# Two state-space convolutions with a gate: units of 64 channels, an inverse turned through DRAM, and a first stage in array quarters

## The chip, the cores and the metric

The kernel runs on one core of a Trainium2 chip. The metric is device time in microseconds of one execution; the median of three runs of the kernel before is 520.16 us (519.94 to 523.69). Profiles are of one execution, recorded by the hardware profiler. Engines are named as in the profile: PE (TensorE), DVE (VectorE), ACT (ScalarE), POOL (GpSimd), and SP, whose queue issues all DMA transfers here.

## What is computed

The input `x` has 2048 time steps and 512 channels, all in fp32. Two diagonal state-space systems, A and B, each with 128 complex states per channel, give a convolution kernel each, and the outputs are mixed by a gate that depends on the time step alone:

```python
P = exp(logdA[:, :, None] * l)             # 512 channels x 128 states x 2048 steps
K = einsum("dn,dnl,dn->dl", Cc, P, dB).real  # system A; system B has 2 * (C dt . P).real
y = irfft(rfft(u, 2L) * rfft(K, 2L))[:L] + u * Dskip
g = sigmoid((x * gate_w).sum(-1))           # one number per time step
out = g * a + (1 - g) * b
```

No library transform exists on the chip, so both kernels `K` are summed up by matmuls over the states, and the convolution is done by a discrete transform in two stages, also of matmuls, with an inverse in two stages.

## The kernel before, in words

The 512 channels are cut into four quarters `q` of 128. A **unit** is one quarter of one system (`k` = 0 for A, 1 for B), so there are eight units. A unit goes through these steps:

- `params_t`, `params_c` (once per quarter): small operations of 128 states x 256 that turn the raw parameters into phases (integers, so that they wrap), decay exponents and a complex factor. Most of it is on DVE, some on ACT and POOL.
- `anchors`, `weights`: ACT fills a table `AB` of exponentials; POOL multiplies part of it by the factor.
- `chunk`, eight times per unit, 16 channels each. POOL makes two phase products in a tile `x` (L562 and L553) and two products of exponentials in a tile `E` (L573, L581). ACT takes four sines and cosines of 128x512 into PSUM banks (L591, L592, L595, L599), with one Abs of 128x1024 between (L593). DVE multiplies them with `E` into `Qt`, `Pt`, `Ct` and `Dt` (L603, L606, L616, L621, L612); for 31 of the 64 chunks `Dt` is made on POOL instead, from a sine in SBUF (`scs`). PE sums over the states (`products`, L638: four column strips of 32), adds the skip tap (L647), and ACT copies the result to `K`.
- stage one (`stage1`, `put`, L681): matmuls of `K` with a small cosine table into `F`, 256 columns at a time in two column halves; a copy by DVE or ACT (L692, L694).
- `stage2`: forward matmuls with `Gw` (L703), a product with the transformed input read back from DRAM as `U` (L764, L767 on DVE), inverse matmuls with `Tw` (L775, L776), and a copy back into `F` by ACT (L781).
- `final`: DVE transposes `F` in place in 32x32 blocks (L797), PE does the last inverse stage (L803), and the result is multiplied by the gate on its way out of PSUM: system A's by ACT or DVE (L817, L819), stored to DRAM as `w0`, and loaded again for system B, where DVE multiplies and adds (L880).

The input itself goes through stage one and the forward matmuls once per quarter (`stage1_u`, `stage2_u`), and its transform is written to DRAM (`ud`). `gate` sums `x * gate_w` by matmuls (L902) and takes the sigmoid.

What sets the order: every operation is recorded with an engine, a cost, a due time and the buffers that it reads and writes. `Plan.run` plays a clock over these costs; whenever an engine is free, the ready operation with the earliest due time goes next. The outcome is a fixed order of instructions per engine, in which they are then written. The numbers at the top of the file (`LAG`, `FSP`, `TO` and so on) shift the due times; `SLOTS` and `CAPS` say how many tiles of each kind there are. Each engine runs its instructions in that order, waiting on semaphores. PSUM has eight banks of 128x512; before, all eight are one pool `ps`, of which the sines may hold four.

## Time and profile before

| | |
|---|---|
| median of three runs | 520.16 us |
| profiled execution, span from first to last instruction | 519.0 us |
| PE busy | 453.8 us, 7732 matmul records |
| DVE busy | 444.5 us, 740 instructions |
| ACT busy | 418.1 us, 786 instructions |
| POOL busy | 423.1 us, 368 instructions |
| moved by DMA | 74.71 MB, 35747 packets |

Every fp32 matmul of the program appears as two records, each with its weight load (PEld). Busy times of the four engines overlap; none says by itself what the span would be without it. A line of the table of groups gives the source line, the engine, the operation, the tiles written and read, the shape and the count, then the busy time and the mean of one, then the idle time of the engine right before these instructions and what ended it.

### The profile page before, as it was taken

What the parts mean: (1) busy time and instruction counts of PE and PEld (TensorE: products, weight loads), DVE (VectorE), ACT (ScalarE), POOL (GpSimd) and SP (SyncE); (2) the same over time, 40 slices, a digit from 0 to 9 for tenths busy, and PEclk for the clock granted to TensorE, in tenths of its full rate; (3) what the DMA queues carried; (4) which work ended last, traced back from release to release, by engine and by line L of the source; (5) the groups of instructions that cost most, each with busy time, mean ns of one, the idle gap of its engine ahead of it and who ended that gap; (6) DMA issues with size and microseconds to landing.
All of it is one profiled execution on the core that took longest, in us unless ns stands there. A gap on an engine that the chain in (4) does not pass through costs nothing.

```text
span 519.0 us, 18350 instructions
## 1 busy us (share of the span) xinstructions
PE 453.8 (87%) x7732; PEld 393.0 (76%) x7732; DVE 444.5 (86%) x740; ACT 418.1 (81%) x786; POOL 423.1 (82%) x368
## 2 busy tenths in 40 slices
PE   2788999879879868979999999996889799999993
PEld 1687989778768646769877898995769679987971
DVE  6658898887959879999999999999998978999854
ACT  4778797797999769989999968876999998675233
POOL 4376999987999998986998999997799989994003
PEclk9879999889969999988999999997899989999999
DMA  8728438624205454435235664440255063433632
GB/s 296 316 74 263 124 105 246 190 88 157 83 3 164 162 180 136 153 103 164 83 124 163 194 221 147 153 124 12 75 158 179 13 215 103 135 123 133 201 116 81
DMA packets 35747, 74.71 MB, mean 144 GB/s; under 512 B 3792, under 2 KB 4176, under 8 KB 35408
## 3 DMA queue, kind: packets, MB, share of 16 engines
q1 hardware_dynamic: 35664, 73.54, 43.7%
q8 instruction: 60, 0.98, 0.8%
q14 instruction: 23, 0.19, 0.1%
HBM read 53.60 MB, written 19.92 MB: 142 GB/s over the span
## 4 chain that ended last, share of the span: by engine, by line
PE 40%; DVE 21%; ACT 20%; issue 6%; DMA 5%; POOL 5%; SPq 0%; POOLq 0%; DVEq 0%; ACTq 0%
PE ps L681 9%; PE ps L703 8%; PE ps L775 7%; PE ps L776 6%; PE ps L638 6%; PE ps L803 3%; ACT AB L496 2%; DMA AB<-in_prm 2%; ACT ps L591 2%; ACT x L593 2%; DVE F L797 2%; DVE Ct L621 2%; DVE Pt L616 2%; DVE z L767 2%; DVE F L692 2%
## 5 line engine op out<-in xcount | busy, mean ns | idle before, releaser
L581 POOL TENSOR_TENSOR E<-AB 128x1024 f32<-128x1024 f32 x64 | 125.2, 1958 | 0.1
L703 PE MATMUL ps<-F,c_g 128*128 128x128 f32 x768 | 105.6, 286 | 15.9 <-DVE fi L453 9.0
L703 PEld LDWEIGHTS ps<-F,c_g 128*128 128x128 f32 x768 | 94.8, 195 | 24.4 <-DVE fi L453 9.5
L775 PE MATMUL ps<-z,c_t 128*128 128x128 f32 x512 | 105.5, 289 | 5.7 <-DVE Pt L616 2.6
L776 PE MATMUL ps<-z,c_t 128*128 128x128 f32 x512 | 101.6, 281 | 0.1
L775 PEld LDWEIGHTS ps<-z,c_t 128*128 128x128 f32 x512 | 79.9, 197 | 13.8 <-DVE z L767 3.4
L562 POOL TENSOR_TENSOR x<-pi,c_tm 128x512 int32<-128x512 int32 x64 | 67.8, 1060 | 20.8 <-ACT ps L595 18.7
L616 DVE TENSOR_TENSOR Pt<-ps,E 128x1024 f32<-128x1024 f32 x64 | 77.8, 1216 | 4.8 <-PE ps L638 2.9
L776 PEld LDWEIGHTS ps<-z,c_t 128*128 128x128 f32 x512 | 79.8, 197 | 0.8 <-DVE z L767 0.7
L681 PE MATMUL ps<-w,K 128*64 128x128 f32 x1024 | 68.9, 284 | 10.2 <-ACT K L657 6.3
L681 PEld LDWEIGHTS ps<-w,K 128*64 128x64 f32 x1024 | 57.6, 141 | 19.5 <-ACT K L657 8.2
L573 POOL TENSOR_TENSOR E<-AB 128x512 f32<-128x512 f32 x64 | 68.4, 1070 | 4.2 <-ACT AB L496 2.4
L638 PE MATMUL ps<-Pt,Ct 128*32 128x64 f32 x2048 | 66.1, 227 | 5.5 <-DVE Ct L621 3.4
L553 POOL TENSOR_TENSOR x<-gh 128x512 int32<-128x512 int32 x64 | 68.3, 1068 | 1.9 <-ACT ps L599 1.8
L593 ACT ACTIVATE x<-x 128x1024 f32<-128x1024 int32 x64 | 67.9, 1061 | 1.7
L638 PE MATMUL ps<-Qt,Dt 128*32 128x64 f32 x2048 | 64.4, 224 | 0.0
L781 ACT COPY F<-ps 128x512 f32<-128x512 f32 x64 | 37.2, 586 | 33.8 <-PE ps L776 28.5
L638 PEld LDWEIGHTS ps<-Pt,Ct 128*32 128x32 f32 x2048 | 47.3, 113 | 18.9 <-DVE Ct L621 5.4
L764 DVE TENSOR_TENSOR z<-ps,U 128x512 f32<-128x512 f32 x64 | 43.5, 680 | 20.1 <-DMA U<-ud 14.0
L496 ACT ACTIVATE AB<-al 128x128 f32<-128x128 f32 (+1 forms) x160 | 55.1, 528 | 1.4 <-DVE ps L452 1.1
L638 PEld LDWEIGHTS ps<-Qt,Dt 128*32 128x32 f32 x2048 | 49.2, 114 | 0.0
L603 DVE TENSOR_TENSOR Qt<-ps,E 128x512 f32<-128x512 f32 x64 | 43.4, 679 | 5.3 <-POOL E L581 3.8
(114 smaller groups left out, 869.5 us busy)
## 6 DMA issues: line engine op xcount, KB each, us to landing
U<-ud SPq DMA_DIRECT2D x64, 512.0 KB, 3.9
ud<-z SPq DMA_DIRECT2D x32, 256.0 KB, 3.5
U<-in_u SPq DMA_DIRECT2D x16, 256.0 KB, 4.0
ud<-z SPq DMA_DIRECT2D x32, 128.0 KB, 3.4
U<-in_uT SPq DMA_DIRECT2D x8, 512.0 KB, 4.1
c_t<-in_c_t SPq DMA_DIRECT2D x1, 3072.0 KB, 14.9
w<-st SPq DMA_DIRECT2D x12, 256.0 KB, 2.6
st<-w SPq DMA_DIRECT2D x12, 256.0 KB, 3.0
```

Source lines behind the costliest of these rows:

```text
L496: A.activation(dst()[..., i], src(), AF.Exp, scale=sg * float(t0 + dt * i))
L553: G.tensor_tensor(xi()[:, :, 1, :].rearrange("n c (a b) -> n c a b", a=4), t[:, :, 0:4].unsqueeze(3).to_broadcast([P, NCK, 4, 8]), t[:, :, ...
L562: lambda: G.tensor_tensor(xi()[:, :, 0, :], d["piv"]()[:, k, ch, 0].unsqueeze(2).to_broadcast([P, NCK, NJ]), tm[:, 0:NJ].unsqueeze(1).to_b ...
L573: G.tensor_tensor(Ev()[:, :, 0, :].rearrange("n c (a b) -> n c a b", a=4), A1()[:, ch, ::-1].unsqueeze(3).to_broadcast([P, NCK, 4, 8]), BB ...
L581: G.tensor_tensor(Ev()[:, :, 1:3, :].rearrange("n c w t -> n c (w t)"), AA()[:, ch].rearrange("n c w a -> n (c w) a").unsqueeze(3).to_broa ...
L593: op("A", 1.02, e, lambda: A.activation(x.t, x.v(dt=I32), AF.Abs), w=[x])
L616: lambda: V.tensor_tensor(qv(Pt), tv(cf).unsqueeze(2).to_broadcast([P, NCK, 2, NJ]), Ev()[:, :, 0:2, :], ALU.mult),
L638: T.matmul(K4[32 * b : 32 * b + 32, g, :], tv(lw)[:, 4 * g + b, :], qv(rw)[:, 4 * g + b].rearrange("n h t -> n (h t)"), start=(lw is Ct an ...
L681: T.matmul(b.t[64 * d : 64 * d + 64, 128 * g : 128 * g + 128], Kv[:, g, :], w1[:, d, :], start=True, stop=True,)
L703: T.matmul(pairs(b.t[:, NCH * mm : NCH * mm + NCH]), Gw[:, 4 * mg + mm, :], Fv(F)[:, :, 4 * mg + mm, :], start=True, stop=True,)
L775: T.matmul(hb.t[:, cs], Tw[:, m, 0:128], Z1.t[:, cs], start=True, stop=False)
L776: T.matmul(hb.t[:, cs], Tw[:, m, 64:192], Z2.t[:, cs], start=False, stop=True)
```

## The change

The planner (`Plan`) stays. What it is given changes throughout:

- **Units.** A unit is now 64 channels of both systems, still 128 columns and still eight units. `U` is loaded for 64 channels and used for both systems: 36 loads of 512 KB where there were 64.
- **Gate.** Since `g*a + (1-g)*b = b + g*(a-b)`, PE subtracts B's kernel from A's while it is still in PSUM (`neg`, L669), and the second half of a unit's columns holds `a-b`. The last inverse stage multiplies B's columns by `w1i` and the others by `wg`, which is `w1i` times the gate for each time step (POOL, L898), and adds both in PSUM. The products with the gate on the way out, and `w0`, are gone; a plain copy goes to the output (L855, L857).
- **Turn.** The result of stage two is copied to `st` and written to DRAM (`wt`, 64 writes), and read back with rows in the order that the last stage needs (L827). The transposes on DVE are gone.
- **Sines.** Each chunk takes one sine and one cosine of 128x1024 over two banks (L606, L608) into two tiles `sd` of two banks each; four banks are left as `ps`. `Dt` is always on DVE, as one product with half of `Qt` (L614); the cosine products are written in place into `E` (L624, L629), which has three tiles where there were two.
- **First stage.** 512 columns of `K` at a time are multiplied in quarters of the array: 32 matmuls of 64 rows and 64 columns into two banks (L692).
- **Last unit.** It is transformed in two halves of 64 columns (`SPLIT`), so that its matmuls of stage two move 64 columns each, and written and read in pieces of 64 elements.
- The parameter steps are shorter by five DVE operations per quarter, with two sign operations on POOL instead; `F` has two tiles and a separate tile `X` in place of three; all of `u` is transformed early, and the gate too; the costs given to the planner are other numbers.

The core of the diff:

```diff
-    "F": (4096, 3), "AB": (28 * NCH, 2), "x": (1024, 2), "E": (1536, 2), "Qt": (1024, 2), "Dt": (512, 2),
...
-    "st": (512, 3), "p": (256, 5), "dtb": (256, 2), "pi": (512, 2), "pf": (256, 2), "al": (256, 3), "fi": (256, 2), "gh": (NCK * HC * 12, 1), "ps": (512, 8),
+    "F": (4096, 2), "AB": (28 * NCH, 2), "x": (1024, 2), "E": (1536, 3), "QD": (1536, 2),
...
+    "st": (512, 2), "p": (256, 3), "dtb": (256, 2), "pi": (512, 2), "pf": (256, 2), "al": (512, 1), "fi": (256, 2), "gh": (768, 1), "ps": (512, 4), "sd": (1024, 2),
-CAPS = {"sc": SC, "kg": KG, "kh": KH, "fb": 8}
+CAPS = {"kg": KG, "kh": KH, "s1": 2, "fb": 4, "pm": 1}
...
+        op("A", 1.06, e, lambda: A.activation(bv(sn), wv(xi()), AF.Sin, scale=SCL), r=[x], w=[sn], func="S")
+        op("A", 1.06, e, lambda: A.activation(x.t, x.v(dt=I32), AF.Abs), w=[x])
+        op("A", 1.06, e, lambda: A.activation(bv(cs), wv(qv(x)), AF.Sin, bias=HALF_PI, scale=-SCL), r=[x], w=[cs], func="S")
...
+        if k == 0:
+            first[0] = op(
+                "T", 0.9, due + CK, lambda: T.matmul(kg.t, neg, K.t, start=False, stop=True), r=[K, negB], w=[kg],
+            )
...
+            for g in range(8):
+                for h in range(2):
+                    for d in range(2):
+                        T.matmul(
+                            bs[h].t[64 * d : 64 * d + 64, 64 * g : 64 * g + 64],
+                            K()[64 * h : 64 * h + 64, 64 * g : 64 * g + 64],
+                            w1[64 * h : 64 * h + 64, d, 64 * h : 64 * h + 64],
+                            start=True, stop=True,
+                        )
...
+                lambda st=st, mg=mg: DMA(
+                    wt_t[v, nm * mg : nm * mg + nm, :, 64 * k0 : 64 * (k0 + nk)].rearrange("m p c -> p m c"),
+                    st.v("p (m c) -> p m c", m=nm, c=64 * nk),
+                ),
```

How the order moves, at three places. First POOL, in the middle of the loop (a chunk is `x`, `x`, `E`, `E`; `gh` and `AB` are small tables that several chunks share). Before:

```order
L562 TENSOR_TENSOR x_72<-pi_100,c_tm 128x16x32
L553 TENSOR_TENSOR x_72<-gh_109 128x16x32
L573 TENSOR_TENSOR E_74<-AB_70 128x16x32
L581 TENSOR_TENSOR E_74<-AB_70 128x16x64
L612 TENSOR_TENSOR Dt_78<-scs_81,E_74 128x512
L562 TENSOR_TENSOR x_71<-pi_100,c_tm 128x16x32
```

And of the change, at the like place:

```order
L575 TENSOR_TENSOR x_71<-pi_92,c_tm 128x16x32
L566 TENSOR_TENSOR x_71<-gh_99 128x16x32
L586 TENSOR_TENSOR E_73<-AB_69 128x16x32
L594 TENSOR_TENSOR E_73<-AB_69 128x16x64
L575 TENSOR_TENSOR x_70<-pi_92,c_tm 128x16x32
L566 TENSOR_TENSOR x_70<-gh_99 128x16x32
```

The four products of a chunk stand as before; `Dt`, which waited for a sine and the chunk's own `E`, no longer stands between two chunks.

Second ACT, at a chunk in the middle (`ps`, `scs` and `sd` take the sines, `x` the phases; L781 and L806 copy out stage two's result). Before:

```order
L591 ACTIVATE ps_117<-x_72 128x512
L592 ACTIVATE scs_81<-x_72 128x512
L593 ACTIVATE x_72<-x_72 128x1024
L595 ACTIVATE ps_110<-x_72 128x512
L781 COPY F_66<-ps_112 128x64x8
L599 ACTIVATE ps_112<-x_72 128x512
```

And of the change:

```order
L607 ACTIVATE x_71<-x_71 128x1024
L608 ACTIVATE sd_105<-x_71 128x1024
L806 COPY st_85<-ps_100 128x512
L606 ACTIVATE sd_104<-x_70 128x1024
L607 ACTIVATE x_70<-x_70 128x1024
L608 ACTIVATE sd_105<-x_70 128x1024
L806 COPY st_86<-ps_102 128x512
L671 COPY K_77<-ps_101 128x512
```

Five instructions of a chunk become three; every sine now goes to the one tile `sd_104` and every cosine to `sd_105`, where the banks changed from chunk to chunk.

Third PE, near its end, in the last unit (L802 and L803 are the inverse matmuls of stage two, L716 the forward ones, L837 and L845 the last stage):

```order
L802 MATMUL ps_101<-z_79,c_t 128x64
L803 MATMUL ps_101<-z_82,c_t 128x64
L716 MATMUL ps_103<-F_67,c_g 128x64 x8
L837 MATMUL ps_102<-X,w1i 64x256 x2
L845 MATMUL ps_102<-X,wg 64x64 x8
L716 MATMUL ps_100<-F_67,c_g 128x64 x8
```

Before, PE's end reads (L775 and L776 are stage two, L803 the last stage):

```order
L775 MATMUL ps_113<-z_85,c_t 128x128
L776 MATMUL ps_113<-z_86,c_t 128x128
L803 MATMUL ps_116<-F_68,c_w1i 64x512 x2
L803 MATMUL ps_111<-F_68,c_w1i 64x512 x2
L803 MATMUL ps_112<-F_68,c_w1i 64x512 x2
L803 MATMUL ps_117<-F_66,c_w1i 64x256 x4
```

Matmuls of stage two now move 64 columns where they moved 128, eight forward ones make a step where four did, and pieces of the last stage, which wait for transfers, stand between the steps.

More of the change, by code (lines that the diff above doesn't have):

```diff
@@ L643, in products @@
+                            start=(w == 0 and gg + ko == 0),
                             stop=False,
                         )
[L646 removed]
+            if odd:
+                c0 = (cc0 - NCK) // 4
                 T.matmul(
[L648 to L653 removed]
@@ L654, in chunk @@
-        first[0] = op("T", 1.06, due + CK, products, r=[Ct, Pt, Dt, Qt, tapB, identB], w=[(kg, kreg)], after=opened)
-        if not last:
-            return
-        op("A", 0.48 if two else 0.27, due + CE, lambda: A.copy(K.t[:, 0:n], kg.t[:, 0:n]), r=[kg], w=[K])
-        c1 = c + 1 - n // 256
-        for i in range(n // 256):
-            stage1_k(q, k, c1 + i, lambda i=i: K.t[:, 256 * i : 256 * i + 256], (K, ((i, i + 1),)), due + CS + 1e-3 * i)
+                    kg.t.rearrange("n (c s) -> n c s", s=NS)[:, :, 31], ident,
@@ new lines, in products @@
+                    tap[:, 2 * q + k, c0 : c0 + 8], start=False, stop=(k == 1),
+                )
+        opened = [first[0]] if odd else ()
+        first[0] = op(
+            "T", 1.1 if odd else 0.95, due + CK, products, r=[E, QD, tapB, identB], w=[(kg, ((odd, odd + 1),))], after=opened,
+        )
+        if not odd:
+            return
+        done[v, k, g // 2] = pl.ops[-1]
+        if k == 0:
+            first[0] = op(
+                "T", 0.9, due + CK, lambda: T.matmul(kg.t, neg, K.t, start=False, stop=True), r=[K, negB], w=[kg],
+            )
@@ L945, in gated_s4_mix @@
     for q in range(NQ):
-        pl.unit = q
         stage1_u(q, UDS[q])
```

809 lines of the change are left out of this document (401 added, 408 removed).

## The prediction

> **What bounds the kernel now.** I read the page's first part, then busy time by stretch, then who waited for whom, then the groups.
>
> ```profile
> PE 453.8 (87%) x7732; PEld 393.0 (76%) x7732; DVE 444.5 (86%) x740; ACT 418.1 (81%) x786; POOL 423.1 (82%) x368
> ...
> PE 40%; DVE 21%; ACT 20%; issue 6%; DMA 5%; POOL 5%; SPq 0%; POOLq 0%; DVEq 0%; ACTq 0%
> ```
>
> Four engines are busy for 81 to 87% of the span, and the chain that ended last runs over all of them. No engine bounds the kernel from end to end, so I cut the span where the chunk loop begins and ends: at POOL's first table operation (11.51 us) and at its last one (472.4 us). The columns of the next rows are PE, PEld, DVE, ACT and POOL busy, then clock, DMA share and GB/s.
>
> ```profile
> 0.00:11.51 11.51, 3.75 (x8) 2.41 (x8) 7.40 (x29) 4.72 (x15) 3.87 (x15) 1.00 0.81 286
> 11.51:472.51 461.00, 411.79 (x7366) 360.42 (x7368) 406.89 (x656) 399.22 (x730) 415.26 (x350) 0.95 0.44 141
> 472.51:519.00 46.49, 38.31 (x362) 30.20 (x358) 30.18 (x57) 14.21 (x44) 3.93 (x3) 0.98 0.42 137
> ```
>
> In the middle 461 us POOL works 415.3 and waits 45.7; the others are at 87 to 89%. POOL is ahead by little, but it opens every chunk, so I write the time as: start, POOL's work, POOL's waits, tail. Its two longest in there, by line and releaser (us in total, times, longest):
>
> ```profile
> POOL x L562 <- ACT ps L595: 18.7, 6, 7.8
> POOL AB L512 <- DVE pf L439: 5.8, 1, 5.8
> ```
>
> The first is a phase buffer `x` that ScalarE had not yet finished with (once for 7.8, while the first tables are made), the second a weight that the parameter chain had not yet delivered, also at the start.
>
> **POOL, the term that counts.** Columns: group, then busy us and mean ns, then idle time right before it.
>
> ```profile
> L612 POOL TENSOR_TENSOR Dt<-scs,E 128x512 f32<-128x512 f32 x31 | 39.8, 1283 | 7.8 <-ACT scs L592 2.7 <-POOL E L581 2.2 <-POOL x L562 1.1
> L465 POOL TENSOR_TENSOR fi<-fi,p 128x256 int32<-128x256 int32 x4 | 2.9, 732 | 5.6 <-DVE fi L453 5.5
> L485 POOL TENSOR_TENSOR al<-al,dtb 128x128 f32<-128x128 f32 x4 | 1.8, 456 | 0.4 <-ACT dtb L359 0.4
> ```
>
> The four big operations of a chunk keep count and size. All 31 `Dt` go to VectorE: -39.8. New are two sign operations of 128x256 per quarter; three quarters' lie in the stretch. Such an operation is not in the trace. The smaller and the equal two-input operation bound it by 0.46 and 0.73; I take 0.73, its own size: +4.4. The gate's weights are 16 products of 128 elements, 0.46 each: +7.3 (0.73 each, for their stepped operands, would make 11.7). Work becomes 415.3 - 39.8 + 4.4 + 7.3 = **387**. With `Dt` goes the idle time before it: 45.7 - 7.8 = **38**, if the rest stays. They are the term I know least; bounds are below.
>
> **VectorE** has to stay beside that.
>
> ```profile
> L797 DVE STREAM_TRANSPOSE F<-F 128x512 f32<-128x512 f32 x64 | 41.7, 690 | 4.9 <-ACT F L781 4.9
> L616 DVE TENSOR_TENSOR Pt<-ps,E 128x1024 f32<-128x1024 f32 x64 | 77.8, 1216 | 4.8 <-PE ps L638 2.9 <-ACT ps L595 1.8
> L612 DVE TENSOR_TENSOR Dt<-ps,E 128x512 f32<-128x512 f32 x33 | 22.5, 681 | 0.0
> L880 DVE SCALAR_TENSOR_TENSOR st<-ps,gs,st 128x128 f32<-128x128 f32 x48 | 13.3, 345 | 0.8 <-DMA st<-w 0.4 <-PE ps L803 0.3
> L449 DVE SCALAR_TENSOR_TENSOR ps<-AB,ps 128x256 f32<-128x256 f32 x4 | 1.7, 428 | 0.1
> ```
>
> The 64 transposes go (-41.7), since the turn is done by writing to DRAM and reading back in another order. `Dt` arrives, but joins the first half of `Qt` in one 1024-element product: 64 x 1.216 in place of 64 x 0.68 and 33 x 0.68, +11.8. Eight fewer stage-one copies of that size, -5.4. The gated additions go (-13.3) and eleven smaller gated products with them, against eleven plain copies, about zero. Five fewer parameter operations per quarter, -8.6. In all about -57. Some 15 transposes, 10 us, lay in the tail, so the stretch goes from 406.9 to about 360.
>
> **ScalarE.**
>
> ```profile
> L593 ACT ACTIVATE x<-x 128x1024 f32<-128x1024 int32 x64 | 67.9, 1061 | 1.7
> L591 ACT ACTIVATE ps<-x 128x512 f32<-128x512 int32 x64 | 38.6, 603 | 6.8 <-DVE z L767 1.7 <-DVE Pt L616 1.3 <-DVE Ct L621 1.2
> L496 ACT ACT_TABLE_LOAD x12 | 15.4, 1283 | 0.2
> ```
>
> 256 sines of 512 elements (0.60 each, 154) become 128 of 1024. A sine over two PSUM banks is not in the trace: the 1024-element Abs gives 1.06, two short sines give 1.21. I take 1.06, the row of its own length: 136, so -18 (0 at the other end). Table loads fall from 34 to 26, -10. The stretch goes from 399.2 to 371. Both engines are off the path while POOL has 387 of work.
>
> **TensorE.** A busy TensorE includes the ends of pipelined matmuls, so I count distances between starts.
>
> ```profile
> 252.17 1.09 PE L681 MATMUL ps<-w,K 128*64 128x128 f32 x16
> 253.19 0.32 PE L638 MATMUL ps<-Pt,Ct 128*32 128x64 f32 x8
> ...
> 254.22 0.30 PEld L647 LDWEIGHTS ps<-dskip,c_id 128*128 128x128 f32 x2
> 254.23 0.39 PE L647 MATMUL ps<-dskip,c_id 128*128 128x4 f32 x2
> ...
> 254.44 0.30 PEld L775 LDWEIGHTS ps<-z,c_t 128*128 128x128 f32 x2
> ...
> 492.52 1.06 PE L703 MATMUL ps<-F,c_g 128*128 128x128 f32 x8
> ...
> 493.42 0.38 PE L775 MATMUL ps<-z,c_t 128*128 128x128 f32 x2
> ```
>
> Stage one of 256 columns takes 1.02 (252.17 to 253.19) for 16 matmul records, and is done 96 times. In quarters, 512 columns are 64 records of 64 columns, 48 times. Bounds: 64 records as dense as the chunk products, which run four column strips at once and need 1.04 for 64 records (253.19 to 254.23); or no gain over now, 2.04. I take 1.05, the row with as many records side by side: 98 becomes 50. Against this stand 16 subtractions `neg` and 16 gate products of 512 full-width columns, each as long as the eight records of L703 (0.90): +29, less the 5 that the gate takes now; and the last unit, done in two halves, whose matmuls move 64 columns through weights of 128. The two records of L647 move only 4 columns, and the next weights still start 0.22 later (254.22 to 254.44), as long as two of L703 take: the weight load sets it. So halving the columns saves nothing, and 96 extra matmuls (two records each, 0.22 a pair) cost 21. Sum: -48 + 24 + 21, no change within a few us.
>
> The Trainium skill ("TensorE: Matmul & The Clock Gate", LDWEIGHTS) says that a weight load takes its columns divided by 1.2 GHz, however many rows it has, 107 ns for 128, and so speaks against this split. The trace agrees, with two loads in 0.22 us. By moving columns alone the time would be 12 us less than the sum below; by the rule the sum stands.
>
> **Start and tail.** The first phase product needs `theta` from VectorE; the change drops the two scalings of the identity ahead of it, so I start at 10. All of `u` is transformed early now: ahead of the first chunk product stand 13 stage-one steps (of 512 columns, 1.05) and 18 forward steps (0.90), where 15 (of 256, 1.02) and 7 stood, 8 us more. POOL may hide it, as it can write three chunks ahead (three `E` tiles, two before), one chunk or 6 us more; the rest of 2 us is within the waits. Behind POOL's last product come four VectorE products (2 x 1.22 + 2 x 0.68 = 3.8), products, tap and `neg` (2.2), a copy and one stage one (1.6); then on TensorE 80 stage-two and 32 forward matmuls at 0.22 (24.6) and three finals, which stream as many columns as the 16 records of L681 do, 1.0 each; then the new round trip.
>
> ```profile
> U<-ud SPq DMA_DIRECT2D x64, 512.0 KB, 3.9
> ...
> w<-st SPq DMA_DIRECT2D x12, 256.0 KB, 2.6
> st<-w SPq DMA_DIRECT2D x12, 256.0 KB, 3.0
> out<-st SPq DMA_DIRECT2D x12, 256.0 KB, 2.9
> ```
>
> Copy 0.6, write 2.6, read 3.0, final 1.0, copy 0.4, out 2.9: 10.5. That is 45.7, with semaphores about **47**, against 46.5 now; 35 if weight loads cost less than I say, 53 if the write and read take double. The Trainium skill ("DMA: Bandwidth & Descriptors", Specifications) puts line rate at pieces of 512 B and more, while the split unit moves 256 B pieces; by it the last two transfers would be the slower ones and the sum up to 6 more. No run here shows it.
>
> ```profile
> DVE z L764 <- DMA U<-ud: 14.0, 11, 2.4
> ```
>
> The other transfers I cost at nothing. `U` is loaded 36 times in place of 64 and mostly serves two steps; but 64 writes to `wt` now stand in SP's queue, each until a ScalarE copy is done, and the `U` loads stand behind them. The cover is the pair of buffers: two steps, at a pace of (387 + 38) / 64 = 6.6 us each, against 3.9. If it fails, each of 36 loads could hold VectorE by the 1.3 us that a late `U` costs now (14.0 us in 11 waits), 46 in all, less than the 65 us that VectorE's 360 leaves in the stretch.
>
> **Sum:** 10 + 387 + 38 + 47 = 482 of span, against 519.0 (11.5 + 415.3 + 45.7 + 46.5). The median of the runs (520.16) lies 1.2 above the profiled span, so **483**.
>
> **Rivals.**
>
> *Faster:* with VectorE and ScalarE relieved, only those waits while the first tables are made remain (5.8, 7.8 and an estimated 4 of smaller ones, 18). That gives 10 + 387 + 18 + 47 + 1 = 463. For it: the `x` waits come from a late ScalarE. Against: fewer PSUM banks for the rest.
>
> *Quarters that don't run side by side:* stage one stays at 2.04 per 512 columns, so the 24 and the 21 stand alone, some 30 of them in the stretch: TensorE 442 busy. It then paces; at 94 to 97% busy the stretch is 456 to 470 and the time 514 to 528, no change or a little slower. Nothing in the trace runs row halves side by side.
>
> *Slower, through the sine tiles:* now the four sines of a chunk have up to four single banks, and freed ones go to anyone; afterwards two tiles of two banks, one for sines and one for cosines, and four banks for all else. ScalarE's next sine waits until two VectorE products (1.9 us) have read the last one, and everything queued ahead of these on VectorE (a stage-two pair, two instructions of 512 elements) delays it; behind the sine stand the copies that free TensorE's banks.
>
> ```profile
> ACT ps L592 <- DVE Ct L621: 4.6, 6, 1.7
> ...
> ACT ps L599 <- DVE F L692: 1.8, 3, 0.7
> ```
>
> Such waits cost little now (4.6 and 1.8). ScalarE has 371 us of work in a stretch of 425, so it decides from 54 us of waits, 0.42 per long sine. From 91 us (0.71 per sine, one 512-element VectorE instruction in front of each) the kernel is no faster than before. At 0.95 (half the time a short, half the time a long product) the stretch is 371 + 122 = 493 and the time 551. For it: the banks are tied up twice as much. Against: VectorE loses 57 us.
>
> **Chances.** Forecast, 463 to 508: 0.54. Faster than that: 0.13. Quarters, 508 to 530: 0.15. Sine tiles, above 525: 0.18. About 1% (5 us) is what a measurement can tell. Below 515 lie the first two and a quarter of the third: 0.71; 515 to 525: 0.06; above: 0.23. The range leaves out 0.05 below 455 and about 0.15 above 530.
>
> **What would show it.** Right: POOL about 400 busy in all and none on `Dt`; its waits near 40; 64 stage-one records in about 1.05; the long sine near 1.06; the last product some 43 us before the end. Wrong: ScalarE idle before L606 or L608 for VectorE products (sine tiles); TensorE above 92% with L692 at 2 us (quarters); VectorE idle for `U` (the queue); a late first product, since all stage one of `u` and the gate now come early.

## The result, and the profile after

The change is **slower**: 543.67 us in the median of 4 runs (540.63 to 546.03), against 520.23 for the kernel before on the same chip; the ratio is 1.042, with a 95% interval of 1.037 to 1.048. The prediction was 483, with a range of 455 to 530. The profiled execution has a span of 544.3 us. The profiles of six experiments (e1, e4, e12, e14, e16, e18) are of executions 4 to 9 us above their own medians, that of the change is 2 above and that of e17 2 below, so stretches of different kernels compare to a few us only; verdicts rest on the medians and on the ratios to the kernel before, which leave single slow executions out.

From the page of the kernel after: busy time of the engines, and the chain that ended last.

```profile
PE 457.1 (84%) x9696; PEld 398.0 (73%) x9696; DVE 398.3 (73%) x559; ACT 388.2 (71%) x597; POOL 396.1 (73%) x358
...
PE 48%; DMA 13%; POOL 11%; DVE 10%; ACT 9%; issue 5%; SPq 2%; DVEq 0%; ACTq 0%; POOLq 0%
```

The work moved as intended: VectorE has 46 us less of it, ScalarE 30, POOL 27; TensorE has 3 more. And the span grew by 25. Busy time by stretch, with the span cut at POOL's first table operation, TensorE's first chunk product (58.5 us) and the end of POOL's last one (469.6). Columns as in the prediction: length; PE, PEld, DVE, ACT and POOL busy; clock; DMA share; GB/s.

```profile
0.00:12.80 12.80, 4.86 (x108) 4.25 (x112) 7.16 (x27) 6.47 (x18) 6.17 (x17) 1.00 0.82 278
12.80:58.50 45.70, 36.00 (x884) 33.16 (x876) 26.04 (x42) 32.59 (x63) 20.77 (x19) 0.85 0.78 268
58.50:469.60 411.10, 354.07 (x7853) 303.77 (x7852) 346.14 (x465) 337.93 (x500) 369.19 (x323) 0.95 0.48 148
469.60:544.30 74.70, 62.21 (x867) 56.77 (x865) 18.96 (x28) 11.25 (x20) 0.00 (x0) 0.90 0.54 147
```

The same cut for the kernel before, whose first chunk product came at 46.6 (the other two rows stand in the prediction):

```profile
11.51:46.60 35.09, 28.06 (x304) 25.34 (x308) 23.06 (x43) 27.82 (x62) 18.78 (x17) 0.85 0.62 221
46.60:472.51 425.91, 383.72 (x7070) 335.08 (x7068) 383.83 (x614) 371.40 (x668) 396.48 (x334) 0.96 0.43 134
```

So the change lost 11.9 us ahead of the first product (58.5 against 46.6), **won 14.8 in the middle** (411.1 against 425.9), and lost 28.2 behind POOL's end (74.7 against 46.5). The prediction's four terms, by the same rows:

| term | predicted | profiled |
|---|---|---|
| start | 10 | 12.8 |
| POOL's work from there to its end | 387 | 390.0 (20.77 + 369.19) |
| POOL's waits | 38 | 66.8 (24.9 before the first product, 41.9 after) |
| tail | 47 | 74.7 |
| span | 482 | 544.3 |

POOL's two longest waits, by line and releaser (us in total, times, longest):

```profile
POOL E L586 <- PE ps L645: 27.4, 10, 12.7
POOL x L575 <- ACT sd L608: 20.5, 13, 6.6
```

The first is new. The cosine products are written into `E` in place, so POOL gets a tile back only when TensorE has read it; 12.7 us of it is the wait for the first chunk product. The tail, cut behind the last chunk product (486.5) and behind the last stage-two matmul (524.2):

```profile
469.60:486.50 16.90, 16.90 (x366) 16.13 (x365) 10.34 (x14) 4.71 (x7) 0.00 (x0) 1.00 0.57 178
486.50:524.20 37.70, 37.70 (x439) 35.88 (x429) 7.35 (x11) 5.59 (x11) 0.00 (x0) 1.00 0.53 148
524.20:544.30 20.10, 7.61 (x80) 4.77 (x80) 1.27 (x3) 0.96 (x2) 0.00 (x0) 0.61 0.53 118
```

TensorE is busy without a gap for 54.6 us after POOL has ended. Its groups in that time, shapes kept apart:

```profile
L803 PE MATMUL ps<-z,c_t 128*128 128x64 f32 x128 | 24.7, 275 | 0.0
L802 PE MATMUL ps<-z,c_t 128*128 128x64 f32 x128 | 24.7, 275 | 0.0
L716 PE MATMUL ps<-F,c_g 128*128 128x64 f32 x123 | 15.2, 274 | 0.0
```

All 128 stage-two matmuls of the split unit (256 records) stand here, its first half too, and nearly all of its forward ones.

The sizes that the prediction had taken, from the groups of the whole execution:

```profile
L802 PE MATMUL ps<-z,c_t 128*128 128x128 f32 x448 | 90.3, 284 | 7.2 <-DVE z L793 5.2 <-DVE z L790 1.6 <-ACT F L704 0.3
...
L692 PE MATMUL ps<-w,K 64*64 64x64 f32 x2048 | 39.2, 225 | 12.0 <-ACT K L671 5.7 <-DVE fi L462 2.5 <-issue 1.3
...
L606 ACT ACTIVATE sd<-x 128x1024 f32<-128x1024 int32 x64 | 66.0, 1032 | 8.3 <-POOL x L566 4.0 <-DVE QD L619 3.9
...
L427 POOL TENSOR_SCALAR p<-AB 128x256 f32<-128x256 f32 x4 | 4.3, 1070 | 1.2 <-DVE ps L379 1.2
```

A record of 64 columns lasts 275 ns, one of 128 columns 284: halving the columns saves next to nothing. The quarters run side by side (32 stage-one steps of `K` in 39.2 us, 1.2 each where 1.05 was counted). The long sine takes 1.03 us, and all 64 of them lose only 3.9 us to VectorE's products. Only the sign operation was far off, 1.07 in place of 0.73.

### The profile page after: what moved, and what is told of

Its sections match the earlier page's. It is cut to its first block, busy times and chain, and to the rows that moved or that the text cites. A ratio compares the mean times of both kernels' runs of the same rounds, so it can differ in the third digit from the quotient of the medians.

```text
span 544.3 us, 22084 instructions
## 1 busy us (share of the span) xinstructions
PE 457.1 (84%) x9696; PEld 398.0 (73%) x9696; DVE 398.3 (73%) x559; ACT 388.2 (71%) x597; POOL 396.1 (73%) x358
## 4 chain that ended last, share of the span: by engine, by line
PE 48%; DMA 13%; POOL 11%; DVE 10%; ACT 9%; issue 5%; SPq 2%; DVEq 0%; ACTq 0%; POOLq 0%
PE ps L716 12%; PE ps L802 9%; PE ps L803 8%; PE ps L645 6%; PE ps L692 5%; DMA ud<-z 3%; POOL E L594 3%; DMA U<-in_u 3%; DMA X<-wt 3%; POOL x L566 2%; ACT sd L606 2%; PE ps L845 2%; POOL x L575 2%; PE ps L837 2%; PE ps L880 2%
## 5 line engine op out<-in xcount | busy, mean ns | idle before, releaser
L802 PE MATMUL ps<-z,c_t 128*128 128x128 f32 (+1 forms) x576 | 115.0, 282 | 7.2 <-DVE z L793 5.2
L803 PE MATMUL ps<-z,c_t 128*128 128x128 f32 (+1 forms) x576 | 112.8, 278 | 0.7 <-DVE z L793 0.3
L802 PEld LDWEIGHTS ps<-z,c_t 128*128 128x128 f32 x576 | 88.7, 193 | 13.4 <-DVE z L793 6.2
L716 PE MATMUL ps<-F,c_g 128*128 128x128 f32 (+1 forms) x704 | 92.7, 278 | 6.5 <-DVE z L751 2.4
L716 PEld LDWEIGHTS ps<-F,c_g 128*128 128x128 f32 x704 | 84.4, 191 | 10.7 <-DVE z L751 2.8
L803 PEld LDWEIGHTS ps<-z,c_t 128*128 128x128 f32 x576 | 88.3, 194 | 1.6 <-DVE z L793 1.6
L586 POOL TENSOR_TENSOR E<-AB 128x512 f32<-128x512 f32 x64 | 68.3, 1069 | 28.3 <-PE ps L645 27.4
L575 POOL TENSOR_TENSOR x<-pi,c_tm 128x512 int32<-128x512 int32 x64 | 67.8, 1060 | 25.0 <-ACT sd L608 20.5
L614 DVE TENSOR_TENSOR QD<-sd,E 128x1024 f32<-128x1024 f32 x64 | 77.9, 1217 | 8.7 <-PE ps L645 3.4
L624 DVE TENSOR_TENSOR E<-sd,E 128x1024 f32<-128x1024 f32 x64 | 77.8, 1216 | 1.6 <-ACT sd L608 1.6
L645 PE MATMUL ps<-E 128*32 128x64 f32 x2048 | 66.4, 227 | 14.3 <-DVE E L624 7.1
L606 ACT ACTIVATE sd<-x 128x1024 f32<-128x1024 int32 x64 | 66.0, 1032 | 8.3 <-POOL x L566 4.0
L608 ACT ACTIVATE sd<-x 128x1024 f32<-128x1024 f32 x64 | 66.1, 1033 | 2.9 <-DVE E L624 1.2
L806 ACT COPY st<-ps 128x512 f32<-128x512 f32 x64 | 37.3, 584 | 43.2 <-PE ps L803 39.4
L645 PEld LDWEIGHTS ps<-E 128*32 128x32 f32 x2048 | 49.3, 112 | 24.6 <-issue 8.6
L645 PE MATMUL ps<-QD 128*32 128x64 f32 x2048 | 65.3, 224 | 0.0
L645 PEld LDWEIGHTS ps<-QD 128*32 128x32 f32 x2048 | 51.3, 113 | 0.0
L692 PEld LDWEIGHTS ps<-w,K 64*64 64x64 f32 x2048 | 34.3, 138 | 20.5 <-ACT K L671 10.0
```

What stands on the lines that cost most here:

```text
L575: lambda: G.tensor_tensor(xi()[:, :, 0, :], d["piv"]()[:, k, ch, 0].unsqueeze(2).to_broadcast([P, NCK, NJ]), tm[:, 0:NJ].unsqueeze(1).to_b ...
L586: G.tensor_tensor(Ev()[:, :, 0, :].rearrange("n c (a b) -> n c a b", a=4), A1()[:, ca, ::-1].unsqueeze(3).to_broadcast([P, NCK, 4, 8]), BB ...
L606: op("A", 1.06, e, lambda: A.activation(bv(sn), wv(xi()), AF.Sin, scale=SCL), r=[x], w=[sn], func="S")
L614: lambda: V.tensor_tensor(ev(QD)[:, :, 0::2, :], bv(sn).rearrange("n w c t -> n c w t"), Ev()[:, :, 0::2, :], ALU.mult),
L624: lambda: V.tensor_tensor(Ev()[:, :, 0:2, :], bv(cs)[:, 0].unsqueeze(2).to_broadcast([P, NCK, 2, NJ]), Ev()[:, :, 0:2, :], ALU.mult),
L645: T.matmul(K4[32 * b : 32 * b + 32, gg, :], ev(QD if w else E)[:, c, 2, :], ev(QD if w else E)[:, c, 0:2].rearrange("n h t -> n (h t)"), s ...
```

## The experiments

### The three places where the change lost time

**The last unit whole again** (e1).

```diff
-SPLIT = (7,)
+SPLIT = ()
```

> The last unit is transformed whole again, as the seven others are: 192 records of 64 columns fewer for TensorE, the rest as in the change (the planner orders it anew). Theory 'TensorE behind' (at POOL's last operation TensorE still has work of the last two units, so what is taken from it there comes off the end one for one): 192 x 0.11 = 21 us, so 522 to 526 us, TensorE busy near 437, POOL's span to within 5 us of the change's, the tail behind POOL 52 to 58 us instead of 75. Rival 'chain' (the halves were there so that one could go early; whole, all of stage two stands behind the last product): no gain, 540 to 548.

Measured: 531.95 us, ratio to the kernel before 1.022 (1.015 to 1.029), 12 us less than the change. By stretch:

```profile
58.10:474.10 416.00, 357.18 (x7913) 306.28 (x7912) 348.12 (x467) 337.12 (x499) 369.19 (x323) 0.95 0.47 147
474.10:534.30 60.20, 41.54 (x612) 35.90 (x612) 16.79 (x25) 11.76 (x21) 0.00 (x0) 0.83 0.46 140
```

TensorE's work falls to 439.2 (17.9 for 192 records, 0.09 each) and the tail by 14.5. The middle is 5 longer, but this profile lies 5 us above its median, so how much of that is the edit's stays open. In the tail, where it had a backlog, TensorE now waits for reads:

```profile
PE ps L837 <- DMA X<-wt: 12.1, 6, 7.1
```

So neither theory holds in full: the split costs, but 12 rather than 21.

**Four read tiles for the last quarter** (e2). `Fq` is four quarters of the tile `X`; the results go to `z`.

```diff
+    pl.tiles["Fq"] = [xt[:, 1024 * i : 1024 * i + 1024] for i in range(4)]
...
-            f, y, o = Buf("Fp"), bank(), Buf("st")
+            f, y, o = Buf("Fq" if nu == 1 else "Fp"), bank(), Buf("z" if nu == 1 else "st")
```

> The last quarter's reads of wt go into four tiles of 1024 elements in place of two of 2048, and its results into four buffers in place of two; nothing else changes up to TensorE's last stage-two matmul. Theory 'two rounds' (the end has two round trips through DRAM one after the other, since only two read tiles exist, where the prediction had one): behind the last stage-two matmul 13 to 15 us in place of 20.1, so 538 us. Rival 'shared transfers' (four reads at once take as long as two after two, since the pieces are of 256 bytes): within 1.5 us of the change, 542 to 545.

Measured: 538.43 us (1.037, 1.029 to 1.044), 5 less, which is hardly clear of the noise (the change has 1.037 to 1.048); the chain shows more. The end of the chain in the change (start, length, what):

```profile
524.86 2.56 DMA wt<-st
...
527.50 3.42 DMA X<-wt
...
530.96 1.15 PE ps L845 x16
...
535.36 3.97 DMA X<-wt
...
539.37 1.15 PE ps L845 x16
```

And with four tiles:

```profile
524.43 3.34 DMA X<-wt
...
527.82 1.12 PE ps L847 x16
528.94 0.85 PE ps L839 x4
529.79 0.85 PE ps L847 x16
```

The second read of 4 us is gone from the chain. Behind the last stage-two matmul stand 16.4 us in place of 20.1, not the 13 to 15 that were expected: "two rounds" holds, at 3.7 us.

**The input's transform cut to one quarter** (e3): the order and everything else stay.

```diff
+        if q:
+            skip.update(pl.ops[n0:])
...
-both(ud_t[q, v % 2, up])
+both(ud_t[0, v % 2, up])
```

> Leaves work out: of the input's transform only the first quarter's is made (24 of 32 forward steps, 12 of 16 stage-one steps, 12 of 16 input loads and 48 writes of ud less), and every quarter uses it; all other instructions stand in the same order as in the change. Theory 'late first product' (POOL's extra waits are those in front of TensorE's first chunk product, which stands behind the input's transform): the first product at 35 to 42 us in place of 58.5, POOL's waits before 60 us under 10 in place of 25, and the whole rest shifted, 522 to 530 us. Rival 'the middle' (POOL would wait for TensorE, ScalarE or transfers later all the same): POOL's waits in all stay above 60 us and the time above 538.

Measured: 532.8 us (1.024, 1.018 to 1.031), 11 less. The first product comes at 36.4, 22 us earlier, and in front of it:

```profile
12.80:36.40 23.60, 15.71 (x228) 14.33 (x221) 13.85 (x23) 17.05 (x31) 19.41 (x17) 1.00 0.75 277
```

POOL waits 4.2 there in place of 24.9. But half of the 22 us does not arrive at the end. The second chunk's product comes 13 us behind the first:

```profile
49.63 0.44 PE L645 MATMUL ps<-E 128*32 128x64 f32 x8 [12.11 <-DVE E L624]
```

From 35.4 to 44.5 ScalarE, in its fixed order, loads tables and fills `AB` before it takes that chunk's sine. In the change the second chunk comes at 66.0, so 16 of the 22 us are left there. The late first product is a cause; but the edit also takes 28 us of TensorE's work away (457.1 to 429.3), and no run moves the product without that.

**Both, whole unit and four read tiles** (e4), the two diffs above.

> Both edits together: the last unit whole, and four read tiles for the last quarter. Theory 'TensorE behind' with 'two rounds': 524 less 4 to 6, 518 to 521 us, level with the kernel before. If the two overlap (the whole unit already leaves fewer pieces to read): 522 to 525.

Measured: 527.0 us (1.011, 1.002 to 1.020), 17 less: the two add up, though not down to the 518 to 521 expected, as the split was worth less than 21.

### Does POOL pace the kernel?

The prediction's sum stood on that. Each of the next kernels leaves out work of one engine and keeps all instructions in their order.

```diff
+            n = NCK // 2 if v else NCK
+            cb = slice(ca.start, ca.start + n)
             G.tensor_tensor(
-                Ev()[:, :, 1:3, :].rearrange("n c w t -> n c (w t)"),
+                Ev()[:, 0:n, 1:3, :].rearrange("n c w t -> n c (w t)"),
```

> The change, with work left out on POOL alone: from the second unit on, POOL's long product (the 128x1024 one, 1.96 us) is made for half of its channels, 128x512 elements, the rest keeps old values; the order of instructions and all other engines' work stay. POOL loses 56 x 0.98 = 55 us of its 396. Theory 'POOL paces', the recorded prediction's sum (start, POOL's work, POOL's waits, tail): 55 us off the end, 489 us, POOL's waits as before. Rival 'POOL waits for the others' (its waits are what is left of its time when TensorE, VectorE and ScalarE hold E and x): 538 to 548 us, and POOL's idle time grows by the 55.

Measured: 541.0 us (1.044, 1.038 to 1.049), level with the change. POOL has 49 us less work, and its waits take it up: by the two stretches before its end they come to 110 us (46.40 - 20.71 + 405.00 - 320.37), against 66.8. Its two longest were 27.4 and 20.5:

```profile
13.10:59.50 46.40, 37.84 (x885) 34.65 (x878) 26.61 (x44) 32.74 (x63) 20.71 (x19) 0.96 0.82 278
59.50:464.50 405.00, 354.25 (x7852) 304.81 (x7852) 342.41 (x463) 337.88 (x500) 320.37 (x323) 0.95 0.48 149
```

```profile
POOL x L575 <- ACT sd L610: 43.3, 18, 6.2
POOL E L586 <- PE ps L647: 34.7, 10, 13.6
```

The same in the kernel before (e7):

> The kernel before, with the same half of POOL's long product left out from the second unit on (55 us of POOL's 423). Theory 'POOL paces': 465 us. Rival 'POOL waits for the others': 512 to 522 us; then POOL did not pace the kernel before either, and the prediction's sum was wrong already where it was made.

Measured: 519.26 us (0.996, 0.993 to 1.000). **POOL paced neither kernel.** A busy share that leads the others by a little says nothing on who waits for whom.

TensorE with half of stage two (e6), and the same in the kernel before (e8):

```diff
-                    T.matmul(o, Tw[:, m, 0:128], zv(Z1), start=True, stop=False)
-                    T.matmul(o, Tw[:, m, 64:192], zv(Z2), start=False, stop=True)
+                    T.matmul(o, Tw[:, m, 0:128], zv(Z1), start=True, stop=True)
```

> The change, with work left out on TensorE alone: of each pair of stage-two matmuls the second is not made (288 matmuls, 576 records, 63 us by 0.22 a matmul); the order and all other engines' work stay. Theory 'TensorE paces one for one': 63 off, 478 to 486 us. Rival 'TensorE sets the time, but the fixed order ties it to the others' (they are at 71 to 73% and hand work to and fro): a part of the 63 comes off, 505 to 530 us, and TensorE's idle time grows. Theory 'POOL paces': 540 or more, apart from what the tail loses (128 of these matmuls stand behind POOL's end, half of them gone: 14 us), so 530.

> The kernel before, with the second of each pair of stage-two matmuls left out (256 matmuls, 56 us of TensorE's 454). Theory 'TensorE paces one for one': 464 us. Rival 'tied to the others' (VectorE 86%, ScalarE 81%, POOL 82% in the kernel before): 500 to 515 us, less than in the change, whose other engines have more room. Theory 'POOL paces': 510 or more (the tail alone gains).

Measured: 518.42 us for e6 (0.997, 0.995 to 1.000), 25 less than the change; 514.45 for e8 (0.990, 0.987 to 0.993), 6 less than the kernel before. In e6:

```profile
58.50:458.90 400.40, 318.15 (x7479) 265.05 (x7478) 345.04 (x464) 336.78 (x501) 369.07 (x323) 0.93 0.49 151
458.90:516.70 57.80, 45.17 (x664) 40.00 (x664) 18.68 (x28) 11.06 (x19) 0.00 (x0) 0.89 0.70 188
```

17 of the 25 come from the tail, where POOL has ended and TensorE has the most to do. In the middle it has 36 us less work and the stretch is 10.7 shorter. e6 lies where "TensorE sets the time, but the fixed order ties it to the others" put it. e8 was expected at 500 to 515 and lies there, but "POOL paces" (510 or more) would allow it too; e7 tells these two apart.

VectorE (e10: the two long products for half of the channels) and ScalarE (e11: the two long sines for half), one line of each:

```diff
-                Ev()[:, :, 0:2, :], bv(cs)[:, 0].unsqueeze(2).to_broadcast([P, NCK, 2, NJ]), Ev()[:, :, 0:2, :], ALU.mult
+                Ev()[:, 0:n, 0:2, :], bv(cs)[:, 0, 0:n].unsqueeze(2).to_broadcast([P, n, 2, NJ]), Ev()[:, 0:n, 0:2, :], ALU.mult
...
-        A.activation(bv(sn), wv(xi()), AF.Sin, scale=SCL)
+        A.activation(bv(sn)[:, :, 0:n], wv(xi())[:, :, 0:n], AF.Sin, scale=SCL)
```

> The change, with work left out on VectorE alone: from the second unit on, the two long products of a chunk (sine by E, cosine by E, 1.21 us each) are made for half of the channels; the rest keeps old values, order and other engines as they were. VectorE loses 67 of 398 us. Theory 'TensorE sets most of the time': 535 to 543 us. Rival 'VectorE's hand-offs do' (TensorE waits for its products and stage-two pairs more than for anything else): 528 or less.

> The change, with work left out on ScalarE alone: from the second unit on, the long sine and the long cosine (1.03 us each) are taken for half of the channels; order and other engines as they were. ScalarE loses 57 of 388 us. Theory 'TensorE sets most of the time': 535 to 543 us. Rival 'ScalarE's copies and sines hold the others': 528 or less.

Measured: 538.7 us for e10 (1.035, 1.030 to 1.041), 5 less for 60 us of work; 542.6 for e11 (1.044, 1.038 to 1.049), 1 less for 45. Both lie in the range of "TensorE sets most of the time", and neither gain is clear of the noise. The middle is 404.9 and 404.6 us long, 6 shorter each.

All three omissions together, TensorE with all of its work (e16):

> The change in its own order, with the three omissions of e5_light_pool, e10_light_dve and e11_light_act together: from the second unit on POOL's long product, VectorE's two long products and ScalarE's two long sines are made for half of the channels; TensorE does all of its work. Alone they shortened the stretch from the first chunk product to POOL's end (411 us) by 6, 6 and 7. Theory 'in turns' (every engine is near its limit somewhere, so that relieving one only hands the limit to the next; with three relieved TensorE alone sets it, 354 us of work in that stretch): the stretch 365 to 385 us, the time 495 to 520. Rival 'hand-offs' (the delays from engine to engine along a chunk set the stretch, whatever the durations): the three add up at most, the stretch 392 or more and the time 525 or more.

Measured: 528.0 us (1.012, 1.007 to 1.017), 16 less for some 150 us of work; the middle is 400.9 long. "In turns" wanted 495 to 520 and 365 to 385, and is out. The rival's bounds hold, but by the time its "at most" does not: alone the three took 3, 5 and 1 off, 9 in sum, each with some 3 us of noise. By the middle it is 10 against 6, 6 and 7, in a profile 8 us above its median. So the three together may give a little more than their sum, and nearly all of the 150 us turns into waits.

**The subtraction on VectorE** (e9), in the same order.

```diff
-                "T", 0.9, due + CK, lambda: T.matmul(kg.t, neg, K.t, start=False, stop=True), r=[K, negB], w=[kg],
...
+        less = lambda: V.tensor_tensor(K.t, kg.t, K.t, ALU.subtract)
+        op("A", 0.59, due + CE, (lambda: A.copy(K.t, kg.t)) if k else less, r=[kg], w=[K])
```

> The change, with B's kernel subtracted from A's by VectorE on the way out of PSUM (16 products of 128x512) in place of TensorE's 16 'neg' matmuls and ScalarE's 16 copies; the same order otherwise. TensorE loses 14.4 us of work, ScalarE 9, VectorE gains 11. Theory 'TensorE sets most of the time, in a fixed order' (0.4 us per us of its work, as the lighter TensorE gave: 25 of 63): 6 off, 535 to 541 us. One for one: 529. If VectorE's hand-offs count as much as TensorE's: 542 to 548.

Measured: 547.4 us (1.056, 1.049 to 1.062), 4 more than the change, in the range of the last theory (TensorE's busy time fell by 9.0, not 14.4). TensorE's wait for `K`, here and then in the change:

```profile
PE ps L691 <- DVE K L669: 14.0, 6, 3.0
```

```profile
PE ps L692 <- ACT K L671: 5.7, 6, 2.8
```

VectorE's queue has other work ahead of the subtraction, and TensorE stands waiting. Work moved to an engine with more free time came back as a wait.

### Order or work?

In the next kernels the planner's order is replaced by a fixed list. The lists were found by moving operations about at random and playing each trial along the queues: every engine takes its operations in order, each waits for what it reads and for a free buffer, with durations of the trace. No time below comes from that.

```diff
-    order = pl.run()
+    order = [pl.ops[i] for i in ORDER]
+    bufs = list(dict.fromkeys(b for o in pl.ops for b in o.bufs))
+    for b, s in zip(bufs, PLACE):
+        if s >= 0:
+            b.t = pl.tiles[b.tag][s]
```

> The change's own 1876 operations, each on the same engine with the same size and operands; only their order on the engines, and which of several equal buffers each one uses, is another (a fixed list in place of the planner's, found by moving operations about and playing the durations of this trace along the queues). Theory 'order' (the engines' queues are fixed, and each engine stands for 70 to 150 us at the head of its queue while later instructions could run): 510 to 532 us, TensorE as busy as before (457) but idle 20 us less or more. Rival 'work and buffers' (four single banks, two sine tiles, E held until TensorE has read it, two read tiles: they tie the engines in whatever order): 538 to 548 us.

> The same with the kernel before: its own operations, in an order found in the same way. If the kernel before stands in a good order and the change in a poor one: 515 to 522 us, no gain. If both have the same slack in their order: 500 to 512 us, and then the change's work has to be compared with this one, not with 520.

Measured: 523.87 us for e12 (1.007, 1.003 to 1.011), **20 less than the change with the same operations**; 507.73 for e13 (0.978, 0.970 to 0.985), 12 less than the kernel before. Both have slack in their order, the change more. In e12 the first product comes at 52.0 and the tail is 63.0 long; the middle, at 411.6, is not shorter. TensorE's idle time fell by 12 us in the profile (526.7 less 451.1, against 544.3 less 457.1), less than the 20 that the theory asked for.

Next, that edit with those of e1 and e2 and with the copies out of PSUM shared anew between VectorE and ScalarE (e14), and with three more (e15), of which two in short:

```diff
-            op("T", 0.9, due + CK, lambda: T.matmul(kg.t, neg, K.t, start=False, stop=True), r=[K, negB], w=[kg])
+            op("V", 0.68, due + CE, lambda: V.tensor_tensor(K.t, kg.t, K.t, ALU.subtract), r=[kg], w=[K])
...
-        op("A", 2.0, d1, lambda: A.activation(gs.t, gs.t, AF.Sigmoid), w=[gs], func="G")
+            op("A", 0.59, d1, lambda y=y, gs=gs: A.activation(gs.t, y.t, AF.Sigmoid), r=[y], w=[gs], func="G")
```

> The change with its last unit whole and four read tiles (527 us in the planner's order), its copies out of PSUM shared anew between VectorE and ScalarE, in an order found in the same way. Theory 'order': 495 to 512 us, faster than the kernel before; TensorE, with 438 us of work, above 86% busy. Rival 'work and buffers': 520 to 530 us.

> As e14_whole_reads_order, with three more edits: B is subtracted on VectorE (TensorE loses 14 us of work, ScalarE 9, VectorE gains 11), the gate's sums go through four short sigmoids from PSUM into z buffers, not before the second unit's first chunk, in place of copies and one long sigmoid, and a quarter's parameter steps stand in a fixed order; the order of instructions is found in the same way. In the planner's order the subtraction gained nothing. Theory 'TensorE's work pays once the order lets it': 4 to 12 us below e14_whole_reads_order. Rival 'VectorE's hand-offs count as much': level with it or up to 5 above.

Measured: 503.91 us for e14 (0.966, 0.959 to 0.974), and 513.57 for e15 (0.986, 0.979 to 0.993), 10 above. Three edits differ between them and each has its own order, so what of the 10 is the subtraction's stays open; that it did not pay agrees with e9.

A longer search for e14's kernel, with longer delays between engines and the share of the copies sought again (e17):

> As e14_whole_reads_order (whole last unit, four read tiles, other order), with an order sought longer and with longer delays between engines. If there was slack left in the order: 492 to 502 us. If what is left is in the work and in delays that the search does not know: 502 to 507, as e14_whole_reads_order.

Measured: **491.71 us** (0.944, 0.939 to 0.948), just under the range for "slack left in the order", and faster than both kernels. Its page and stretches:

```profile
PE 424.0 (87%) x9504; PEld 369.2 (76%) x9504; DVE 400.7 (82%) x567; ACT 394.4 (81%) x597; POOL 396.1 (81%) x358
```

```profile
17.80:42.70 24.90, 21.01 (x480) 19.65 (x480) 19.67 (x34) 23.69 (x49) 20.86 (x18) 1.00 0.70 213
42.70:432.60 389.90, 352.09 (x8122) 303.22 (x8123) 353.18 (x478) 348.75 (x507) 369.03 (x323) 0.99 0.55 168
432.60:487.50 54.90, 40.93 (x645) 37.57 (x643) 17.71 (x27) 12.44 (x23) 0.00 (x0) 0.91 0.62 189
```

Against the change: 16 us earlier to the first product, 21 in the middle, 20 behind it (POOL's last operation ends at 431.6, 1 us ahead of the cut). POOL's waits for ScalarE's cosines are down from 20.5 us in all to this:

```profile
POOL x L707 <- ACT sd L740: 4.7, 4, 3.4
```

And the kernel before, with the same effort (e18):

> The kernel before in an order sought as long and with the same longer delays as in e17_order2, its copies out of PSUM shared anew between VectorE and ScalarE as there (it was 508 in the shorter search). If the change's design, without its three costs, is the better one once both stand in a good order: 500 to 508 us, 8 to 16 above e17_order2's 492. If the gain was in the order alone: 488 to 496, level with it.

Measured: 497.47 us (0.954, 0.951 to 0.956), between the two ranges. Of the 28 us between e17 and the kernel before, 23 are to be had without the change, by another order and another share of the copies. For the change's design, with its last unit whole and four read tiles, about 6 are left, or 1%. That rests on one search each, and the longer search took 12 us off e14, so these 6 can be the search's as well.

## Why the prediction was wrong

**The form of the sum failed first.** "POOL is ahead by little, but it opens every chunk, so I write the time as: start, POOL's work, POOL's waits, tail." Its work was forecast well (387, measured 390.0). But POOL's waits were not a small rest that "stays": they are the time that POOL has left while the others hold `E` and `x`. Take 49 us from its work and the waits grow by 44 (e5); in the kernel before it was the same (e7). What `Dt` freed on POOL therefore bought next to nothing, and so did what VectorE and ScalarE lost (e10, e11, e16). The trace held a number against it. The kernel before, behind its last stage-two matmul:

```profile
504.30:519.00 14.70, 6.66 (x45) 2.98 (x44) 7.43 (x12) 6.27 (x25) 3.93 (x3) 0.94 0.19 72
```

TensorE idles there for 8.0 us, and for 14.8 ahead of the first chunk product. With its 453.8 us of work, for which I forecast "no change within a few us", that is 477. My 482 left it 5 us of waits in between, where it had 42 (519.0 less 453.8, 14.8 and 8.0) and has 57 after the change. This is an estimate and no hard floor: the busy time itself moves with the order (441.1 in e13 for the same 7732 records).

**The tail, 47 predicted and 74.7 measured,** failed in three terms. I let TensorE have caught up when POOL ends: 3.8 us until the last product, measured 16.9. TensorE is busy for all of it, and the others stand behind it. The last chunk's cosine follows two copies in ScalarE's queue that wait for TensorE, so its last operand is ready 12 us after POOL's end:

```profile
474.87 0.59 ACT L671 COPY K<-ps 128x512 f32<-128x512 f32 x1 [3.22 <-PE ps L669]
478.39 0.58 ACT L806 COPY st<-ps 128x512 f32<-128x512 f32 x1 [2.93 <-PE ps L803]
478.87 1.03 ACT L608 ACTIVATE sd<-x 128x1024 f32<-128x1024 f32 x1
...
480.54 1.22 DVE L624 TENSOR_TENSOR E<-sd,E 128x1024 f32<-128x1024 f32 x1
```

Behind the last product I counted "80 stage-two and 32 forward matmuls" and three finals, 31.4; measured 37.7. And the round trip of 10.5 was run twice, since only two read tiles exist and the next reads waited behind an output in SP's queue: 20.1 (16.4 in e2). The rule that the weight load sets the time of a 64-column matmul was right, and so was its price within a sixth (17.9 us for 192 records, against 21); what I did not draw from it is that half of a split unit costs as much behind POOL's end as a whole one, so the split can win nothing there (e1: 12 us).

**"8 us more. POOL may hide it"**: the first product came 11.9 us later, and POOL's waits ahead of it rose to 24.9 (from 16.3), since the third `E` tile is held until TensorE has read it. The 8 was near (TensorE's busy time ahead of the product grew by 9.0); that POOL would hide it was not. e3 gives 11 us back without this work.

These three (12, 5 and 11 us in e1, e2 and e3) are more than the 23 by which the change is slower; by their sum it would be about where the kernel before is without them. No run undoes all three, and e3 leaves work out.

**Right:** VectorE and ScalarE were not the bound, and the forecast of their work in the stretch was near (VectorE 372 against 360, ScalarE 371 against 371); the quarters run side by side; sines over two banks cost 1.03 and hardly wait; `U` held VectorE nowhere among its longer waits. The gate and the subtractions on TensorE took 17.2 and 17.5 us of busy time, where 14.4 each had been counted. Of my rivals none came true. The signs that I named for "wrong" held one that did: "a late first product". Times above 525 got 0.23 in all, for other mechanisms: the sine tiles, which were to decide there, cost the long sines 3.9 us.

**Not settled:** why the middle shortens by 6 to 11 us whichever engine is relieved, and by 21 in e17's order. The order is shown to be one cause; how far delays between the engines are another, no run separates.

## What to carry to other kernels

Where four engines are 70 to 88% busy in fixed queues, take no engine for the pace because its share is the highest: halve its work in place and look whether the end moves. An edit that frees time on three engines and leaves the busiest as it was has, roughly, that one's work plus its unavoidable idle time as its floor; forecast from there, and count the order of the queues as a cost of its own, here worth more than the whole change of design. Work that is cut finer to start earlier gains only if it does start earlier and if the pieces cost less than the whole.

## What the runs showed of the hardware

**The granted clock differs between orders of the same matmuls.** e1 and e17 have the same 9504 records; TensorE is busy for 439.2 us at a mean granted clock of 0.943 in the one and 424.0 at 0.979 in the other, 414 and 415 by the product (409 and 413 in e4 and e14, with as many records). In the change itself:

```profile
340.00:360.00 20.00, 15.53 (x224) 13.02 (x225) 15.64 (x26) 16.77 (x32) 16.79 (x15) 0.83 0.60 199
360.00:380.00 20.00, 20.00 (x550) 17.58 (x549) 17.95 (x25) 18.73 (x32) 18.65 (x16) 1.00 0.31 97
```

The lower clock stands in the row with gaps. Gaps alone do not bring it about: the first row of e3 above (15.71 busy of 23.60) and that of e17 (21.01 of 24.90) show 1.00. The Trainium skill ("TensorE: Matmul & The Clock Gate", Part 1: The HAM clock gate) says that the gate halves the clock after an idle window of some 3.4 us and opens after as long a busy one. The two rows agree in direction; no run isolates one window. TensorE's busy time is 15 us less in e17 than in e1; how much of e17's gain that makes is not shown.

**One product of VectorE takes 0.43 or 3.85 us, by what POOL does beside it.** `L452` multiplies two operands that both lie in SBUF, four times in the execution; its likes read at least one from PSUM and take 0.43. In the profile after, VectorE's rows (start, length) at its first two, and POOL's beside the second:

```profile
18.02 0.43 DVE L452 TENSOR_TENSOR ps<-p,fi 128x256 f32<-128x256 f32 x1
134.55 3.85 DVE L452 TENSOR_TENSOR ps<-p,fi 128x256 f32<-128x256 f32 x1
```

```profile
133.32 3.77 POOL L898 TENSOR_TENSOR wg<-X,w1i 128x128 f32<-128x128 f32 x9
137.04 1.06 POOL L575 TENSOR_TENSOR x<-pi,c_tm 128x512 int32<-128x512 int32 x1
```

At 18.0 POOL has just stopped; at 134.6 it works without a gap until 138.1, and the product ends at 138.4, as if it had run only then. The Trainium skill ("SBUF — State Buffer", SBUF: two separate sides) says that a VectorE instruction with two SBUF inputs and a GpSimd instruction take one pair of ports by an exclusive lock. The rows agree; no run separates it. Here it costs VectorE 4.6 us in all, and the longest of the four stands on the chain that ended last.

**Pieces of 256 bytes cost the round trip less than the prediction allowed for.** The prediction gave up to 6 us by the Trainium skill ("DMA: Bandwidth & Descriptors", Specifications). The last write of `wt`, in such pieces, took 2.56 us and the read behind it 3.42, against 2.6 and 3.0 for the transfers of as many bytes in the kernel before. The eight such reads took 4.0 in the median, and the second one on the chain 3.97. So a round trip lost about 1 us; no run separates the size of the pieces from the other traffic.
